# Zero products accumulated onto open PSUM groups at the end of the attention head, those groups spread further, and two reorderings

## The chip, the cores and the metric

The kernel runs as one program on one core of a Trainium2 chip. The metric is the device time of the execution in microseconds (us). The core has five engines with instruction streams of their own: TensorE (PE in the profile, with its weight loads as PEld), VectorE (DVE), ScalarE (ACT), GpSimd (POOL) and SyncE (SP), which here only issues transfers. Each engine takes its instructions in the order of its stream, and semaphores order the engines among each other.

## The reference

Three layers follow each other: causal attention with a decay bias over 2 batches of 8 heads (576 positions, head size 64), a leaky two-matrix MLP over the 1152 tokens (512 to 2048 to 512), and four small experts whose outputs are weighted and summed.

```python
scores = scale * np.matmul(q, k.transpose(0, 1, 3, 2))
cum = np.cumsum(np.maximum(s, 0.0), axis=-1)
bias = -(cum[:, :, :, None] - cum[:, :, None, :])
scores = np.where(causal, -1000000000.0, scores + np.minimum(bias, 0.0))
attn = softmax(scores)                      # written out in the original
x = np.matmul(attn, v)                      # to (1152, 512)
h = x @ w_in
x = np.maximum(0.01 * h, h) @ w_out         # to (1152, 512)
for e in range(4):
    out += p[:, e:e + 1] * (np.maximum(x @ w1[e], 0.0) @ w2[e])
```

The weights `w_in` and `w_out` come as 64-bit numbers and are converted to 32 bits on the chip.

## The kernel before

**Order of the work.** Every instruction goes through a small wrapper (`issue`, line 43, which is why nearly every row of the profile reads L43). While its flag `fixed` is true, the instructions stay in the order in which the Python code is run; after the line `fixed = False` a scheduler may reorder them.

**The head.** Attention is cut into 16 units, each two heads of one batch and either the first two tiles of 128 queries (units 0 to 7, "the head") or the last three (units 8 to 15). The generator `attention` counts items `i` (one tile of one head), and each item passes through five steps with lags: `scores` (products into `ps_sc`, then a DVE reduction into `z` and `mn`), `exps` (ACT, lag 1), `transposes` (PE into `ps_pt`, then an ACT copy to `pv`, lag 3), `values` (PE into `ps_o`, after the unit's last item the DVE's `st` and `xo`, lag 5) and `finish` (PE into `ps_x`, then ACT and DVE into `x0`, lag 7). `ps_o` has one buffer, so the next unit's first `values` waits for the `xo` of the unit before. Between the steps the loop weaves other work: while `i < 20` two products of a zero tile (`idling(2)`, into a bank `nothing` of their own); from `i = 22` one step of `opening` at a time, three products of 512 columns of the first MLP into one of three `ps_u` banks that stay open over four rounds; and `units_of_w`, the conversion of the weights on ACT and DVE (`raw`, `w`). The head's loop ends when unit 7 is finished, at `i = 38`. `split_keys` (`qs`, `ks`, `kd`) prepares the keys of units 8 to 15 on ACT and DVE.

**First loads.** `cumulative` issues the first transfers on SP: the row of `s`, keys and queries of units 0 and 1, their values `vs`, and the two rows of the cumulated sum (`decay`, `ke<-cum`), one for each of the two halves `l` of its split.

**The MLP in two sets of tokens.** The first MLP is done for the first 512 tokens (`phases[0]`, woven into the attention) and then for the other 640 (`phases[1]`, the second set), in four blocks each. A block has two up steps and one down step, in the order that `in_order` gives. In the second set an up step (`paired_up`) forms 4x4 blocks of a product from 7 products in place of 8: its weights are a "seven" (`w7`, made by POOL sums, an ACT copy as the high part and a POOL difference as the low part; two buffers), its results fill four PSUM banks, which ACT and DVE turn into the hidden tile `ht`. A down step (`down1`) has 8 groups of 12 products of 320 columns into `ps_d`, with two weight tiles `w` (three buffers). Two sevens are made ahead of the second set. The order of the steps there is up b0 first, up b0 second, up b1 first, down b0, up b1 second, up b2 first, down b1, and so on. This stretch is scheduled, not fixed.

Of the kernel before, what the change touches and what calls it, by code (L numbers as in the profile page):

```python
# [9 lines left out]
F32 = mybir.dt.float32  # L10
# [9 lines left out]
def attention_moe_moe2(ctx: ExitStack, tc: tile.TileContext, q, k, v, s, w_in, w_out, probs, w1, w2, out):  # L20
# [30 lines left out]
    B, H, D, S = q.shape  # L51
# [3 lines left out]
    P = 128  # L55
# [19 lines left out]
    def f32(ap):  # L75
        return ap.bitcast(F32)
# [161 lines left out]

    def in_order(blocks):


        for i in range(len(blocks) + 1):
            if i < len(blocks):
                yield "up", blocks[i], 0
            if i > 0:
                yield "down", blocks[i - 1], None
            if i < len(blocks):
                yield "up", blocks[i], 1

# [63 lines left out]
    def opening(h):  # L313

        w = next_w(2)
        ps = [ps_mm.tile([P, 512], F32, tag="mm", name="ps_u") for _ in range(3)]
        for kk in range(KD):
            for i in range(3):
                wi, sl = w[i // 2], slice(i % 2 * P, (i % 2 + 1) * P)
                for j, (l, m) in enumerate(((0, 0), (1, 0), (0, 1))):  # L320
                    nc.tensor.matmul(ps[i], wi[:, l, kk, sl], x_t[0][:, m, kk], start=(kk == j == 0), stop=(kk == KD - 1 and j == 2))
                if kk == KD - 1:
                    evict_up(ps[i], h)
                yield
        yield from up1(w[1], h, (1,))
# [162 lines left out]
    ps_mm = banks.enter_context(tc.tile_pool(name="ps_mm", bufs=3, space=PSUM))  # L488
# [9 lines left out]
    cum2 = nothing = None  # L498
    idle = ap.tile([P, P], F32, name="idle", bufs=1)
# [3 lines left out]
    def cumulative():  # L503

        nonlocal cum2
        pos, cum = (r64p.tile([P, 2048], F32, tag="r64", name=n)[:BH] for n in ("pos", "cum"))
        spos, zero, cum = pos[:, :S], pos[:, S : 2 * S], cum[:, :S]
        nc.sync.dma_start(spos, s)
        nc.vector.memset(idle, 0.0)
        nc.vector.memset(zero, 0.0)  # L510
        idling(22)
        load_keys(0)
        load_values(0)
        load_keys(1)
        cum2 = early.tile([BH, 2, S], F32R, name="cum2")
        for lo, hi in ((0, half[0]), (half[0], S)):
            part = slice(lo, hi)
            nc.vector.tensor_scalar(spos[:, part], spos[:, part], 0.0, D ** 0.5, ALU.max, ALU.mult)
            nc.vector.tensor_tensor_scan(cum[:, part], spos[:, part], zero[:, part], cum[:, lo - 1 : lo] if lo else 0.0, ALU.add, ALU.add)
            nc.scalar.copy(cum2[:, 0, part], cum[:, part])  # L520
            nc.vector.tensor_tensor(cum2[:, 1, part], cum[:, part], f32(cum2[:, 0, part]), ALU.subtract)
            if lo == 0:
                decay(0, k_e[0])
                load_values(1)
                decay(1, k_e[1])
        nc.sync.dma_start(cum_d.rearrange("l h k -> h l k"), f32(cum2))

    def idling(n):

        for _ in range(n):  # L530
            nc.tensor.matmul(nothing[:, :P], idle, idle, start=True, stop=True)


    v_s = [ap.tile([P, QT, 2 * D + 2], F32, tag=f"v{i}", name="vs", bufs=1) for i in range(4)]
# [53 lines left out]
    def load_values(n):  # L588
        b, hp, i0, i1 = of_unit(n)
        q1, rows, vs = tiles[i1 - 1][2], slice(hp * P, (hp + 1) * P), v_s[n % 4]  # L590
        full = min(q1 // P, QT - 1)
        nc.sync.dma_start(vs[:, :full, 1 : 2 * D + 1], v[b, : full * P, rows].rearrange("(t p) c -> p t c", p=P))
        if i1 == QT:
            nc.sync.dma_start(vs[P - S % P :, QT - 1, 1 : 2 * D + 1], v[b, full * P :, rows])
# [19 lines left out]
    def decay(n, kd):  # L614

        b, hp, i0, i1 = of_unit(n)
        q1, h = tiles[i1 - 1][2], b * H + 2 * hp
        if n < 2:
            for l in range(2):
                nc.sync.dma_start(kd[D + l : D + l + 1], f32(cum2[h : h + 2, l, :q1]))  # L620
        else:
            nc.sync.dma_start(f32(kd[D:DK, :, :q1]), cum_d[:, h : h + 2, :q1])

# [88 lines left out]
    def attention():  # L712

        nonlocal ending
        items, starts, n = [], {}, 0
        i, split = 0, iter(())
        while n < units or i < len(items) + 7:
            if n < units and i == len(items):
                u = Unit(n)
                starts[n] = i  # L720
                items += [(u, *of) for of in u.items]
                if n + 2 < units and n + 2 != 2 * NP:
                    load_keys(n + 2)
                    if n + 2 < 2 * NP:
                        decay(n + 2, k_e[(n + 2) % 3])
                if n + 3 == 2 * NP:
                    load_keys(n + 3)
                n += 1
            if n < units - 1 and i == starts[n - 1] + 2:
                load_values(n + 1)  # L730
            if i == starts[n - 1] + 2 and 2 * NP - 1 <= n < units and n != 2 * NP:
                split = split_keys(max(n, 2 * NP))
            for step, lag in STEPS:
                if 0 <= i - lag < len(items):
                    u, *of = items[i - lag]
                    ending = step == Unit.exps and 0 <= i - 5 < len(items) and items[i - 5][1:] == items[i - 5][0].items[-1]
                    step(u, *of)
                if lag == 1:
                    next(split, None)
                if lag in (1, 3, 7):  # L740
                    yield i
            i += 1
# [9 lines left out]
    with ExitStack() as phase:  # L752
        x_t[0] = phase.enter_context(tc.tile_pool(name="x0pool", bufs=1)).tile([P, 2, KD, sizes[0]], F32R, name="x0")
        wpool = phase.enter_context(tc.tile_pool(name="wpool", bufs=4))
        r64p = phase.enter_context(tc.tile_pool(name="r64p", bufs=2))
        side, units_of_w, late, opened = attention(), supply(), late_splits(), 0
        nothing = ps_mm.tile([P, 512], F32, tag="mm", name="nothing")
        with tc.tile_pool(name="early", bufs=1) as early:
            ones = pads(early)
            cumulative()  # L760
            main = mlps(phases[0])

            for at_ in range(3 * 64):
                i = next(side)
                if done == 2 * NP:
                    break
                if at_ % 3 == 0 and i in (6, 8):
                    nc.scalar.copy(q_s[i // 2 - 3][D:DK, 1], ones[D:DK])
                if at_ % 3 == 1:
                    if i < 20:  # L770
                        idling(2)
                    elif i >= 22 and opened < 3 * (done // 2) and (opened < 6 or i >= 30):
                        next(main)
                        opened += 1
                if at_ % 3 == 2:
                    if i in (1, 5):
                        fetch64(i // 4)
                    if i >= 8 and (i < 21 or i >= 29):
                        next(units_of_w)
        hidden_pool(phase, 6)  # L780

        owed = 0
        for at_, i in enumerate(side):
            if at_ % 3 < 2:
                owed += WOVEN * KD / (2.0 * (48 - 6))
                while owed >= 1.0:
                    next(main)
                    owed -= 1.0
            if at_ % 3 != 1:
                next(late, None)  # L790
            if at_ % 3 == 2 or at_ % 3 == 0 and not ending:
                next(units_of_w, None)
        attn.close()
        w7pool = ctx.enter_context(tc.tile_pool(name="w7pool", bufs=2, side="right"))
        scratch = ctx.enter_context(tc.tile_pool(name="scratch", bufs=2, side="right"))
        t7pool = ctx.enter_context(tc.tile_pool(name="t7pool", bufs=1, side="right"))
        tokens = paired_steps(1, x_t[1], t7pool)
        banks.close()
        ps_mm = ctx.enter_context(tc.tile_pool(name="ps_all", bufs=8, space=PSUM))

        sevens = first_sevens()
        for m, _ in enumerate(main):
            if m % 2 == 0:
                next(late, None)
            if m % 4 == 0:
                next(tokens, None)
            if m % 4 == 2:
                next(units_of_w, None)
            if m % 4 % 2 and m >= 4:
                next(sevens, None)  # L810
        for _ in sevens:
            pass
        for _ in tokens:
            pass
# [57 lines left out]
```

## Time and profile before

| What | Value |
|---|---|
| Time, median of 3 runs | 746.86 us (744.03 to 746.86) |
| The profiled execution: its own time, its span | 739.91 us, 738.1 us |
| Mean granted TensorE clock over the span | 0.992 of 2.4 GHz |
| PE busy | 715.0 us, 97% of the span |
| PEld, DVE, ACT, POOL busy | 88%, 58%, 45%, 39% |
| Chain that ended last | PE 87%, DVE 5%, ACT 3%, issue 2% |

The profiled execution is 1.8 us longer than its span, and 7 us shorter than the median of the unprofiled runs. PE is the engine that is busy nearly everywhere; its idle time sits in the first 250 us and at one place behind 257 us.

### The profile page before, as it was taken

Reading aid. Unit: us, or ns where it says so; the run is one execution under the profiler, and the core shown is the slowest. Engines: PE = TensorE matmul, PEld = TensorE weight load, DVE = VectorE, ACT = ScalarE, POOL = GpSimd, SP = SyncE. Lnnn points to the kernel's source line nnn. Section 1 sums busy time; section 2 is a strip of 40 time slices with the busy share of each in tenths; the row PEclk is TensorE's granted clock in tenths of the full one; section 3 lists DMA queues with packets and bytes.
Section 4 is the critical chain, followed back from the end, with each engine's and each line's share of the span. In section 5 each row is a group of like instructions: output and inputs, shape, how many; then the busy total and the mean of one; then the engine's idle time right before and its main releaser. Section 6 shows DMA issues by size and latency. Waiting matters only on the chain.

```text
span 738.1 us, 11412 instructions
## 1 busy us (share of the span) xinstructions
PE 715.0 (97%) x4388; PEld 650.6 (88%) x4388; DVE 428.2 (58%) x866; ACT 330.8 (45%) x643; POOL 286.7 (39%) x234
## 2 busy tenths in 40 slices
PE   9998899999999989999999999999999999999997
PEld 9886788888888889999988988989889898898986
DVE  4858797889737735853874544634436444454442
ACT  5767978786654556453531422413324133132210
POOL 4111121211228788885163372522714327053200
PEclk9999999999999999999999999999999999999999
DMA  6775567765432222131020110202103011020012
GB/s 167 216 217 152 158 195 239 247 212 184 169 114 87 87 86 86 58 115 58 1 87 30 57 59 18 69 29 58 57 1 86 29 58 58 0 58 1 1 38 90
DMA packets 40745, 68.85 MB, mean 93 GB/s; under 512 B 3988, under 2 KB 22964, under 8 KB 40692
## 3 DMA queue, kind: packets, MB, share of 16 engines
q1 hardware_dynamic: 31988, 42.97, 19.7%
q10 hardware_dynamic: 8704, 25.17, 9.9%
q8 instruction: 34, 0.56, 0.3%
q14 instruction: 19, 0.16, 0.1%
HBM read 57.30 MB, written 10.82 MB: 92 GB/s over the span
## 4 chain that ended last, share of the span: by engine, by line
PE 87%; DVE 5%; ACT 3%; issue 2%; DMA 1%; ACTq 0%; DVEq 0%; SPq 0%
PE ps_d L43 40%; PE ps_u L43 34%; PE ps_o L43 5%; PE ps_sc L43 3%; PE ps_pt L43 3%; DVE raw L43 2%; PE nothing L43 2%; DMA raw<-w_f 1%; DVE t L43 1%; ACT pv L43 1%; ACT ps_u L43 1%; PE ps_x L43 1%; DVE z L43 0%; ACTq L43 0%; ACT ht L43 0%
## 5 line engine op out<-in xcount | busy, mean ns | idle before, releaser
L43 POOL TENSOR_TENSOR w<-raw,w 128x1024 fp32r<-128x1024 f32 (+2 forms) x88 | 147.5, 1693 | 395.7 <-ACT w L43 395.7
L43 PE MATMUL ps_u<-t,w 128*128 128x320 f32 (+1 forms) x1680 | 237.5, 299 | 4.1 <-ACT w L43 3.0
L43 PEld LDWEIGHTS ps_u<-t,w 128*128 128x128 f32 x1680 | 233.5, 190 | 8.3 <-ACT w L43 3.5
L43 PE MATMUL ps_d<-w,ht 128*128 128x512 f32 x864 | 203.3, 391 | 0.0
L43 PEld LDWEIGHTS ps_d<-w,ht 128*128 128x128 f32 x864 | 160.2, 188 | 31.9
L43 ACT ACTIVATE ht<-ps_u 128x320 fp32r<-128x320 f32 (+2 forms) x176 | 74.1, 432 | 159.6 <-DVE ps_u L43 129.1
L43 PE MATMUL ps_d<-ht,w 128*128 128x320 f32 (+1 forms) x576 | 111.4, 343 | 0.9 <-DVE y L43 0.9
L43 DVE SCALAR_TENSOR_TENSOR oacc<-ps_d,pn,oacc 128x512 f32<-128x512 f32 x63 | 47.3, 751 | 104.3 <-PE ps_d L43 104.3
L43 ACT CAST w<-raw 128x1024 fp32r<-128x1024 f32 (+2 forms) x88 | 63.9, 756 | 87.1 <-PE ps_d L43 71.5
L43 PEld LDWEIGHTS ps_d<-ht,w 128*128 128x128 f32 x576 | 92.1, 191 | 6.7 <-ACT t L43 1.3
L43 PEld LDWEIGHTS ps_o<-vs,pv 128*128 128x128 f32 x480 | 64.2, 193 | 13.1 <-issue 6.4
L43 DVE TENSOR_TENSOR ps_u<-ps_u,tmp 128x320 f32<-128x320 f32 (+1 forms) x120 | 56.4, 471 | 26.7 <-PE ps_u L43 25.3
L43 DVE SCALAR_TENSOR_TENSOR ht<-ps_u,ht 128x320 fp32r<-128x320 f32 (+1 forms) x128 | 56.3, 452 | 23.3 <-ACT ht L43 22.0
L43 PE MATMUL ps_o<-vs,pv 128*128 128x65 f32 x480 | 63.7, 269 | 6.2 <-issue 3.9
L43 DVE TENSOR_TENSOR tmp<-ps_u,tmp 128x320 f32<-128x320 f32 (+1 forms) x80 | 36.9, 464 | 47.4 <-PE ps_u L43 40.5
L43 POOL TENSOR_TENSOR w<-sums,w 128x1024 fp32r<-128x1024 f32 x24 | 58.8, 2451 | 9.5 <-ACT w L43 9.5
L43 PE MATMUL ps_u<-x,w 128*128 128x512 f32 x192 | 57.4, 414 | 0.0
L43 ACT ACTIVATE z<-z,mn 128x256 f32<-128x256 f32 (+4 forms) x80 | 48.6, 608 | 16.6 <-DVE mn L43 15.0
L43 DVE CUSTOM_DVE_ANT_0 z<-ps_sc,mask 128x256 f32<-128x256 f32 (+4 forms) x80 | 40.8, 512 | 20.5 <-PE ps_sc L43 14.1
L43 ACT COPY pv<-ps_pt 128x512 f32<-128x512 f32 (+3 forms) x96 | 38.9, 423 | 19.8 <-PE ps_pt L43 19.4
L43 PE MATMUL ps_pt<-ident,z 128*128 128x128 f32 x240 | 41.6, 282 | 5.5 <-ACT pv L43 5.5
L43 DVE TENSOR_TENSOR ht<-ps_u,ht 128x320 fp32r<-128x320 f32 (+1 forms) x48 | 26.4, 555 | 31.0 <-ACT ps_u L43 30.9
(72 smaller groups left out, 624.9 us busy)
## 6 DMA issues: line engine op xcount, KB each, us to landing
raw<-in_moe_w_dram SPq DMA_DIRECT2D x32, 512.0 KB, 3.5
raw<-w_f SPq DMA_DIRECT2D x25, 512.0 KB, 4.2
r<-in_moe_w_in_dram ACTq DMA_DIRECT2D x8, 1024.0 KB, 8.8
w_f<-raw ACTq DMA_DIRECT2D x16, 512.0 KB, 3.0
r<-in_moe_w_out_dram ACTq DMA_DIRECT2D x8, 1024.0 KB
qr<-in_q_dram SPq DMA_DIRECT2D x16, 160.0 KB, 4.2
kr<-in_k_dram SPq DMA_DIRECT2D x8, 288.0 KB, 8.5
vs<-in_v_dram SPq DMA_DIRECT2D x8, 256.0 KB, 4.9
```

The lines of the kernel that those rows point to most:

```text
L43: ins = call(*args, **kw)
```

## The change

There are five edits. (1) From `i = 31` to the head's end, each item gets two products of the zero tile (`onto_held`), added with `start=False` to the open bank of `opening`'s third group, so that they add zero to what it holds. (2) The nine steps of `opening` that fall into the head's loop are issued at the items of a table `OPENED` in place of at 22 to 27 and 31 to 33. (3) In the second set, the down step of block 0 comes ahead of the first up step of block 1. (4) The values of units 0 and 1 are loaded behind the rows of the cumulated sum. (5) The second row of each of these goes out on ACT's queue.

```diff
     def in_order(blocks):
         for i in range(len(blocks) + 1):
+            down = [("down", blocks[i - 1], None)] if i > 0 else []
+
+            if i == 1 and blocks[0][2] == 1:
+                yield from down
+                down = []
             if i < len(blocks):
                 yield "up", blocks[i], 0
-            if i > 0:
-                yield "down", blocks[i - 1], None
+            yield from down
             if i < len(blocks):
                 yield "up", blocks[i], 1
...
-        ps = [ps_mm.tile([P, 512], F32, tag="mm", name="ps_u") for _ in range(3)]
+        ps = held[:] = [ps_mm.tile([P, 512], F32, tag="mm", name="ps_u") for _ in range(3)]
...
         load_keys(0)
-        load_values(0)
         load_keys(1)
...
             if lo == 0:
-                decay(0, k_e[0])
-                load_values(1)
-                decay(1, k_e[1])
+                for n in range(2):
+                    decay(n, k_e[n])
+                    load_values(n)
...
+    def onto_held():
+
+        nc.tensor.matmul(held[2][:, :P], idle, idle, start=False, stop=False, skip_group_check=True)
...
-            for l in range(2):
-                nc.sync.dma_start(kd[D + l : D + l + 1], f32(cum2[h : h + 2, l, :q1]))
+            for l, queue in enumerate((nc.sync, nc.scalar)):
+                queue.dma_start(kd[D + l : D + l + 1], f32(cum2[h : h + 2, l, :q1]))
...
+        OPENED = (22, 23, 25, 27, 28, 30, 32, 34, 36)
...
-                    elif i >= 22 and opened < 3 * (done // 2) and (opened < 6 or i >= 30):
+                    elif opened < len(OPENED) and i >= OPENED[opened] and opened < 3 * (done // 2):
                         next(main)
                         opened += 1
+                if at_ % 3 < 2 and i >= 31:
+                    onto_held()
```

**The second set, PE's stream.** Before, behind the last six products of block 0's second up step (`ps_u3_2791`, weights `w7_2613`), stand the first products with the third seven (`w7_2708`), and then those of the down step (`ps_d`, weights `w_2783`).

```order
L43 MATMUL ps_u3_2791<-t7_1_2488,w7_2613 128x320 x5
L43 MATMUL ps_u0_2859<-t7_1_2488,w7_2708 128x320 [waits DVE_49,Activation_49]
L43 MATMUL ps_u1_2860<-t7_1_2488,w7_2708 128x320 [waits DVE_49,Activation_49]
L43 MATMUL ps_u2_2861<-t7_1_2488,w7_2708 128x320 [waits DVE_49]
L43 MATMUL ps_u3_2862<-t7_1_2488,w7_2708 128x320 [waits DVE_49]
L43 MATMUL ps_d_2952<-ht_2715,w_2783 128x320 [waits DMAHW4_49,DMAHW0_49,DMAHW6_49,DVE_49,PE_49]
L43 MATMUL ps_d_2952<-ht_2715,w_2783 128x320 [waits Pool_49]
```

With the change the same place (now `ps_u3_2798`) is followed by the down step alone, on the hidden tiles `ht_2722` and `ht_2793` of block 0; its 96 products stand there without a product of an up step among them.

```order
L43 MATMUL ps_u3_2798<-t7_1_2504,w7_2629 128x320 x5
L43 MATMUL ps_d_2888<-ht_2722,w_2719 128x320 [waits DMAHW4_49,DMAHW6_49,DMAHW0_49,DVE_49]
L43 MATMUL ps_d_2888<-ht_2722,w_2719 128x320 [waits Pool_49]
L43 MATMUL ps_d_2888<-ht_2722,w_2719 128x320 [waits DVE_49]
L43 MATMUL ps_d_2902<-ht_2722,w_2719 128x320 [waits Activation_49]
L43 MATMUL ps_d_2902<-ht_2722,w_2719 128x320
L43 MATMUL ps_d_2916<-ht_2722,w_2719 128x320 [waits DVE_49]
L43 MATMUL ps_d_2916<-ht_2722,w_2719 128x320 x2
```

Four product rows with the third seven have gone from there. Three up steps in a row now stand behind the down step: with the seven `w7_2868`, with `w7_2880`, and with the third, `w7_3017`, which takes the buffer of the first. The last products with `w7_2868` are those of `ps_u3_3029`; PE's stream of the change goes on behind them:

```order
L43 MATMUL ps_u2_3099<-t7_1_2504,w7_2880 128x320 x6
L43 MATMUL ps_u3_3100<-t7_1_2504,w7_2880 128x320 x6
L43 MATMUL ps_u0_3097<-t7_1_2504,w7_2880 128x320 [waits Activation_49]
L43 MATMUL ps_u0_3097<-t7_1_2504,w7_2880 128x320 x5
L43 MATMUL ps_u0_3168<-t7_1_2504,w7_3017 128x320 [waits DVE_49,Activation_49]
L43 MATMUL ps_u2_3099<-t7_1_2504,w7_2880 128x320 [waits DVE_49]
L43 MATMUL ps_u2_3099<-t7_1_2504,w7_2880 128x320 x5
L43 MATMUL ps_u3_3100<-t7_1_2504,w7_2880 128x320 [waits DVE_49]
L43 MATMUL ps_u3_3100<-t7_1_2504,w7_2880 128x320 x5
L43 MATMUL ps_u1_3169<-t7_1_2504,w7_3017 128x320 [waits Activation_49]
L43 MATMUL ps_u2_3170<-t7_1_2504,w7_3017 128x320
L43 MATMUL ps_u3_3171<-t7_1_2504,w7_3017 128x320 [waits DVE_49]
```

18 products of the second seven stand between the last product with the first and the first with the third, and 12 more ahead of the next; the row behind these is the first that waits for POOL's low part of the third seven. From the down step of block 1 on, the streams of all engines are those of before but for names.

**The head, PE's stream, items 30 to 32.** Before, from the last `values` of item 30 on (`ps_x` is the `finish` of unit 5):

```order
L43 MATMUL ps_o<-vs,pv 128x65 x2
L43 MATMUL ps_x<-ident,xo 128x128 x2
L43 MATMUL ps_sc<-ke_116,qe_115 128x128
L43 MATMUL ps_pt<-ident,z 128x128 x2
L43 MATMUL ps_u<-x_102,w 128x512 x3
L43 MATMUL ps_o<-vs,pv 128x65
L43 MATMUL ps_sc<-ks,qs 128x448
```

With the change, the same stretch:

```order
L43 MATMUL ps_u<-x_102,w 128x512 x3
L43 MATMUL ps_o<-vs,pv 128x65 x2
L43 MATMUL ps_x<-ident,xo 128x128 x2
L43 MATMUL ps_sc<-ke_116,qe_115 128x128
L43 MATMUL ps_u<-idle 128x128
L43 MATMUL ps_pt<-ident,z 128x128 x2
L43 MATMUL ps_u<-idle 128x128
L43 MATMUL ps_o<-vs,pv 128x65
L43 MATMUL ps_sc<-ks,qs 128x448
```

The step of `opening` that stood behind `ps_pt` of item 31 has moved ahead of the `values` of item 30, and the zero products (`ps_u<-idle`) stand around `ps_pt`. There are 16 of them in all, two in each of the items 31 to 38. Steps now stand at items 34 and 36 as well.

## Rows read from the trace of the kernel before

In the rows of windows the columns are the stretch and its length, the busy time of PE, PEld, DVE, ACT and POOL (with instructions), the granted clock as a share of 2.4 GHz, the DMA share and GB/s. In the rows of the timeline they are start, duration, engine, operation, tiles, shapes and count, with the idle time before and what ended it in brackets. A float32 product of the zero tile, a transpose or a product of `ps_o` shows as two records.

**Rows 1.** Windows of 10 us.
```profile
60.00:70.00 10.00, 7.16 (x38) 5.29 (x37) 9.04 (x17) 8.21 (x16) 2.98 (x1) 0.83 0.83 242
250.00:260.00 10.00, 7.85 (x53) 7.43 (x51) 7.09 (x16) 6.09 (x16) 5.28 (x3) 1.00 0.34 105
260.00:270.00 10.00, 9.16 (x52) 9.09 (x52) 0.99 (x3) 5.10 (x12) 9.18 (x10) 0.83 0.35 107
```

**Rows 2.** Waits of PE over the span: us in total, times, longest.
```profile
PE ps_pt L43 <- ACT pv L43: 5.5, 7, 1.7
```

**Rows 3.** Timeline of PE at the beginning of the second set.
```profile
245.03 12.48 PE L43 MATMUL ps_u<-t,w 128*128 128x320 f32 x84
259.66 0.41 PE L43 MATMUL ps_u<-t,w 128*128 128x320 f32 x1 [2.15 <-ACT w L43]
260.91 0.71 PE L43 MATMUL ps_u<-t,w 128*128 128x320 f32 x3 [0.84 <-ACT w L43]
261.45 4.02 PE L43 MATMUL ps_d<-ht,w 128*128 128x320 f32 x17
```

**Rows 4.** Windows of 1 us with a lower granted clock.
```profile
51.00:52.00 1.00, 1.00 (x6) 1.00 (x6) 0.07 (x2) 0.16 (x1) 0.00 (x0) 0.50 0.91 234
...
263.00:264.00 1.00, 1.00 (x6) 1.00 (x5) 0.49 (x1) 0.02 (x1) 1.00 (x1) 0.50 0.58 123
```

**Rows 5.** Timeline of ACT at the same place.
```profile
257.64 0.43 ACT L43 ACTIVATE ht<-ps_u 128x320 fp32r<-128x320 f32 x1
...
259.00 0.92 ACT L43 CAST w<-raw 128x512 fp32r<-128x512 f32 x2
259.81 1.05 ACT L43 CAST w<-sums 128x1024 fp32r<-128x1024 f32 x1
```

**Rows 6.** Timeline of POOL around the second set's beginning.
```profile
234.57 1.87 POOL L43 TENSOR_TENSOR sums<-sums,raw 128x256 f32<-128x256 f32 x1
...
262.03 2.38 POOL L43 TENSOR_TENSOR w<-sums,w 128x1024 fp32r<-128x1024 f32 x1
264.37 1.98 POOL L43 TENSOR_TENSOR w<-raw,w 128x512 fp32r<-128x512 f32 x2
266.29 1.45 POOL L43 TENSOR_TENSOR sums<-raw 128x256 f32<-128x256 f32 x2
```

**Rows 7.** Timeline of DVE, the sums of tokens for later sevens.
```profile
278.30 0.94 DVE L43 TENSOR_TENSOR sums<-y 128x256 f32<-128x256 f32 x1
...
280.71 1.02 DVE L43 TENSOR_TENSOR t<-y,t 128x512 fp32r<-128x512 f32 x2
```

**Rows 8.** Timeline of PE in the head, where it waited.
```profile
49.82 0.63 PE L43 MATMUL ps_o<-vs,pv 128*128 128x65 f32 x4 [1.84 <-issue]
...
58.71 0.49 PE L43 MATMUL ps_sc<-ks,qs 128*128 128x512 f32 x1 [0.75 <-DVE mn L43]
...
64.22 1.26 PE L43 MATMUL ps_pt<-ident,z 128*128 128x128 f32 x5 [1.72 <-ACT pv L43]
...
68.46 1.30 PE L43 MATMUL ps_o<-vs,pv 128*128 128x65 f32 x10 [0.82 <-PE ps_pt L43]
```

**Rows 9.** The chain in order of time: start, us, what.
```profile
27.92 0.45 PE nothing L43 x4
...
55.25 0.69 PE ps_u L43 x3
```

**Rows 10.** Timeline of DVE in the head.
```profile
49.30 0.42 DVE L43 TENSOR_TENSOR xo<-ps_o,st 128x256 f32<-128x256 f32 x1
...
61.11 0.42 DVE L43 TENSOR_TENSOR x<-ps_x,x 128x256 fp32r<-128x256 f32 x1 [0.83 <-ACT x L43]
```

**Rows 11.** Timeline of PE at the start.
```profile
1.06 7.66 PE L43 MATMUL nothing<-idle 128*128 128x128 f32 x44 [1.06 <-DVE idle L43]
8.56 0.60 PE L43 MATMUL ps_sc<-ke,qe 128*128 128x256 f32 x2
```

**Rows 12.** Timeline of SP's queue at the start.
```profile
5.78 1.41 SPq L43 DMA_DIRECT2D ke<-cum  x2
```

More of the change, by code (lines that the diff above doesn't have):

```diff
@@ L531, in idling @@
             nc.tensor.matmul(nothing[:, :P], idle, idle, start=True, stop=True)
+    held = []
+    def onto_held():
+        nc.tensor.matmul(held[2][:, :P], idle, idle, start=False, stop=False, skip_group_check=True)
     v_s = [ap.tile([P, QT, 2 * D + 2], F32, tag=f"v{i}", name="vs", bufs=1) for i in range(4)]
```

## Prediction, made before the changed kernel ran

> **What bounds the kernel now.** I read the page first: PE is busy for 97% of the span, so only idle time of PE, a clock below full, or added or removed products can move the end. The slices then show where PE idles: in the first 250 us and once behind 257 us. From 270 us on its slices are full; time saved at 257 us reaches the end one for one, since nothing behind it offers slack.
>
> The windows of 10 us show that place with its price: PE busy for 7.85 of 250 to 260, then 9.16 of 260 to 270 at a granted clock of 0.83 [rows 1]. The timeline of PE says what happens. 84 products of block 0 take 12.48 us, 0.149 us each, and end at about 257.5. The next product needs the high part of the third seven and waits 2.15 us for ACT; the one behind it waits 0.84 us for the copy of its sums; the down step begins only at 261.45 [rows 3]. ACT's timeline says why it is late: the hidden tiles of block 0 and other copies stand ahead of those two copies, which start at 259.00 and 259.81 [rows 5]. So the stretch from 257.53 to 261.45 holds 3.92 us and four products (0.59 us): 3.33 us lost. After it the granted clock falls: 0.83 over 260 to 270 is 1.7 us lost [rows 1], with 0.50, which is 1.2 GHz, in the window at 263 [rows 4]. In all the place costs **5.0 us**.
>
> The other place is the head. From item 31 on (about 58 us) PE waits for DVE and ACT in turn, 0.75, 1.72 and 0.82 us in the rows shown [rows 8]; over the span its waits for `pv` come to 5.5 us in 7 places [rows 2]. The clock falls twice: at about 50.9 for some 3.1 us (three windows, of which one is shown, near 0.50 [rows 4]: 1.6 us of work), behind the wait of 1.84 us at 49.8 [rows 8], and at 64.3 for 3.3 us, behind the wait of 1.72 us (0.83 over 60 to 70 is 1.7 us [rows 1]). But in the head DVE is the engine that is busy for 9.04 of 10 us, against 7.16 of PE [rows 1], so neither fall costs its whole 1.6 or 1.7 us.
>
> **The second set's order (edit 3).** It adds and removes no work. Behind the 84 products there are now 96 products of the down step in a row, 14.3 us. Their weights were cast before; of the hidden tiles only the last parts are open. The stream's first such wait is for the ACT tile that starts at 257.64 and takes 0.43 us [rows 5], reached after three products at 257.98: a wait of some 0.1 us, and I allow 0.2. The later tiles have 6 products or more between them, and ACT and DVE have at this place the work that they had. So the 3.33 us go but for 0.2, and with the idle time, which went ahead of the fall of the clock, I take the fall as gone: 3.33 + 1.70 - 0.2 = **4.8 us gained**. The lower bound is 3.1 us (the clock falls later all the same).
>
> What is late next? Three up steps now follow each other. The third takes the buffer of the first seven, so ACT can copy its high part only after the last product with that one. By the stream this is product 150 from the start of the down step, at 257.7 + 150 x 0.149 = 280.0; the new high part is wanted 18 products, 2.7 us, later, the copy of the sums 12 products behind that (1.9 us with the step's own), and the low part of POOL at product 184, at 285.1. ACT needs 0.92 and 1.05 us for its two copies [rows 5], which fits. POOL is closer. It comes free at 264.41 [rows 6] and has in its stream, ahead of that last low part, two halves' low parts (1.98 each time), two sets of sums (four of 0.73, 2.9 each) and three full low parts (2.4 each) [rows 6], in all 17.0 us: 281.4, with an estimated 1.8 us of waiting for ACT's copies 283.2. The slack is 1 to 2 us. I cost this at nothing in the likeliest case; without the cover it is the first rival.
>
> **The head (edits 1 and 2).** The zero product is priced by its kin: the chain shows 0.45 us for four records, two products, so **0.22 us each** at full clock [rows 9]; 16 of them are 3.6 us, and 7.1 us at half clock. An opening step is three products, 0.69 us [rows 9]; there are nine before and after, so moving them adds nothing by itself. Most of the zero products lie in idle time of PE: the three waits shown behind item 31 are 3.3 us [rows 8]. Those that don't are the ones ahead of a `finish`. DVE's `x` at 61.11 waits 0.83 us for ACT's copy of `ps_x` [rows 10], so whatever stands ahead of `ps_x` there is on the path: two zero products, 0.45 us, and the same once more at unit 7's `finish`, another 0.45 us. On the gaining side, two steps fewer stand ahead of the wait at 49.8, but that wait is for DVE's `xo`, which starts at 49.30 whatever PE does [rows 8, 10]; it stays. If the first fall of the clock disappears I count 0.3 us of its 1.6, the part for which DVE had no work of its own; the second is free, since PE waits for DVE again at 68.46 [rows 8]. Sum: 0.45 + 0.45 - 0.3 = **0.6 us lost**. Bounds: both falls disappear and all of it comes back, 0.9 - 3.3 = 2.4 us gained; or the first fall stays and the step that now stands ahead of `ps_x` of item 30 runs at half clock, 2 x 0.69 = 1.4 us more on the path: 2.0 us lost.
>
> **First loads (edits 4 and 5).** PE's idle products run to 8.72 and the first scores start at 8.56 without a wait [rows 11]. What the change shortens is SP's queue, where the two rows `ke<-cum` take 1.41 us [rows 12]: nothing waits for their issue as long as PE has its idle products. I take 0; without that cover it is at most half the row, 0.7 us. The Trainium skill ("DMA: Bandwidth & Descriptors", Issuing engines are not separate DMA queues) says that transfers issued from several engines share the same 16 DMA engines, so that only the issuer's time is saved; by that the edit brings those 0.7 us and no bandwidth, and no run here shows more yet.
>
> **Sum.** -4.8 + 0.6 + 0 = -4.2 us. The profiled execution took 739.91 us itself, so 735.7; it stands 6.95 us under the median of the runs shown, a difference that I can't explain from the trace and carry along. Against the median: 746.86 - 4.2 = **742.7 us**, 0.56% less.
>
> **The rivals.**
>
> *A, as above:* 742.7 us. Chance 0.45.
>
> *B, the third seven is late.* DVE's sums of tokens, from 278.30 to 281.73 before [rows 7], follow the down step, and so run earlier in the change, beside POOL's sums. Where both worked before, one of POOL's sums took 1.87 us in place of 0.73 [rows 6]. With two to three such stretchings POOL is 2.3 to 3.6 us later and eats the 1 to 2 us of slack. PE then waits some 2.4 us at product 184: 742.7 + 2.4 = 745.1, and 746.8 if the clock falls there as it did at 262. Against it: only a few operations of DVE meet POOL's. Chance 0.18. The Trainium skill ("SBUF — State Buffer", Who interferes with whom) speaks for this rival: a VectorE operation with two SBUF inputs shuts out a GpSimd one that reads SBUF for its whole length; the sum of 1.87 us agrees.
>
> *C, the other side: the zero products stand on the head's path.* They wait in PE's order for nothing, but what is behind them (transposes and values for ACT and DVE) waits for them. The point of decision is 4.8 / 16 = 0.30 us a product: at full clock (0.22 us, 3.6 us) the change still gains 1.2 us, at half clock all 7.1 us on the path make 746.86 - 4.8 + 7.1 = 749.2, slower. For it: the clock has been at half at this very place [rows 1, 8]. Against it: PE idles there for 3.3 us. Chance 0.12.
>
> *D, the head gains too.* The zero products fill the idle time that goes ahead of both falls, the clock stays up, and the transposes and values come sooner to DVE and ACT: -4.8 - 2.4 = -7.2, 739.7 us. For it: both falls come behind a wait of over 1.7 us [rows 8]; against it: DVE's 9.04 of 10 us [rows 1], and that the wait at 49.8 lies ahead of the first zero product. Chance 0.25.
>
> **How the numbers follow.** The likeliest is A, 742.7, by itself 741.5 (half of what D would bring the head) to 744.4 (the place at 257 by its lower bound). The range 738.0 to 747.5 holds A, B and nearly all of D; it leaves out C and some of D and B, about 2 in 10. A difference of 0.5% (3.7 us, 743.1) is about what a measurement of this kernel tells from no change, its runs spread over 2.8 us. Faster by more than that: D almost whole, 0.24, and six in ten of A, which straddles the bound, 0.27, with 0.02 of B: 0.53. Slower by more than 0.5%: most of C, 0.09. The rest, 0.38, lies within.
>
> **What would show it right or wrong.** In the changed trace PE should go from `ps_u` to `ps_d` at about 257 us with no wait over 0.3 us, and the windows behind it should read 1.00 in the clock; if a fall stands there or later, 1.7 us of the gain are gone. At the first product with the third seven's low part, some 27 us behind, a wait for POOL's or ACT's `w` shows B. In the head, the start of PE's last `ps_x` and the first opening steps behind the loop, compared with before, give edits 1 and 2 directly: 0.6 us later is A, 2 us earlier is D, 3 us later is C. `ps_sc` at 8.56 should not move. The prediction fails most easily if the head's timing follows PE more than DVE's busy share lets me think, or if some wait far behind the second set takes back what the place at 257 gives.

## The result, and the profile after

The change is faster: 738.27 us median of 10 executions (736.34 to 740.89) against 745.63 of 10 before (739.5 to 747.28), ratio 0.9908 with a 95% interval of 0.9882 to 0.9933, that is 6.9 us or 0.92%. The forecast was 742.7, in a range of 738.0 to 747.5: the result lies 0.3 us inside the range's lower end, and nearer to rival D (739.7) than to the forecast.

The profiled execution of the change took 740.89 us, the longest of the ten, and that of before 739.91, nearly the shortest. Their spans (739.1 and 738.1 us) can't be compared as wholes; their stretches can.

**The second set.** The timeline of PE after the change (start, duration, tiles, shapes, count, and idle time in brackets, of which there is none here) answers to [rows 3]:

```profile
250.71 12.49 PE L43 MATMUL ps_u<-t,w 128*128 128x320 f32 x84
263.04 14.45 PE L43 MATMUL ps_d<-ht,w 128*128 128x320 f32 x96
277.32 13.92 PE L43 MATMUL ps_u<-t,w 128*128 128x320 f32 x93
291.08 4.42 PE L43 MATMUL ps_d<-ht,w 128*128 128x320 f32 x29
```

The 84 products run into the 96 of the down step, and these into the three up steps, with no row of waiting. In the windows (columns as in [rows 1]; the first two are the head's) PE is busy throughout from 260 on, and the clock is at 1.00, which is 2.4 GHz:

```profile
60.00:70.00 10.00, 7.64 (x54) 6.95 (x54) 7.93 (x15) 8.66 (x15) 2.86 (x1) 1.00 0.62 206
70.00:80.00 10.00, 9.08 (x68) 8.37 (x66) 7.95 (x21) 6.27 (x12) 0.00 (x0) 1.00 0.27 65
...
260.00:270.00 10.00, 10.00 (x69) 9.80 (x68) 6.30 (x13) 8.49 (x21) 6.74 (x5) 1.00 0.41 139
270.00:280.00 10.00, 10.00 (x71) 10.00 (x70) 5.94 (x7) 5.33 (x10) 8.76 (x8) 1.00 0.18 65
```

From the first of the 84 products to the end are 738.1 - 245.03 = 493.1 us before [rows 3] and 739.1 - 250.71 = 488.4 after: **4.7 us** gained here. The profiled executions of the experiments agree: this stretch takes 488.4 to 489.3 us in all eleven that have edit 3 and 492.9 to 493.1 in the three that don't, 4.3 us apart in the mean.

**The head.** The same 84 products begin 5.7 us later in the profiled change, and the last `ps_x` of the head, the prediction's own sign, starts at 75.15 against 71.76 before: 3.4 us later, where 0.6 was to be A and 3 was to be C. So these two executions say that everything ahead got slower. The waits of PE, for [rows 2]:

```profile
PE ps_pt L43 <- ACT pv L43: 9.9, 7, 2.9
```

2.7 us of that is one wait that before doesn't have at this place. The timeline of ACT shows its cause, a load of queries that came late:

```profile
45.65 0.72 ACT L43 CAST qs<-qr 128x640 fp32r<-128x640 f32 x1 [2.88 <-DMA qr<-in_q_dram]
```

PE's wait in the profiled change, and in another profiled execution of it (e11, below), whose 84 products begin at 248.93:

```profile
46.59 0.44 PE L43 MATMUL ps_pt<-ident,z 128*128 128x128 f32 x2 [2.72 <-ACT pv L43]
...
46.08 0.44 PE L43 MATMUL ps_pt<-ident,z 128*128 128x128 f32 x2 [0.91 <-ACT pv L43]
```

Its length is that execution's own, its place is not: of the profiled executions with the first six steps of `opening` moved, eight of nine wait here, 0.35 to 2.72 us, and of the five with them at the old items none does. There one more step stood ahead of these transposes, which suggests that edit 2 lets PE arrive before ACT, held up by the queries, has copied `pv`. The start of PE is as it was, the first scores 0.12 us earlier than in [rows 11]:

```profile
1.06 7.54 PE L43 MATMUL nothing<-idle 128*128 128x128 f32 x44 [1.06 <-DVE idle L43]
8.44 0.60 PE L43 MATMUL ps_sc<-ke,qe 128*128 128x256 f32 x2
```

One execution of each kernel doesn't decide what the head gained: the stretch from the last `ps_x` to the 84 products, the work of which no edit changes, takes from 173 to 180 us in the profiled executions. But every timed execution comes with its span and its mean granted clock, and (1 - clock) x span is the work, in time at full clock, that PE could not do. Where PE would have waited anyway, none of it reaches the end. In the profiled execution of before (0.992) that is 5.9 us; over 84 timed ones of before that ran beside the experiments it is 9.9 us on average, from 3.7 to 14.2. The experiments are read by this.

### The profile page after: what moved, and what is told of

Same layout as the page of the kernel before. It is cut to its first block, busy times and chain, and to the rows that moved or that the text cites. A ratio compares the mean times of both kernels' runs of the same rounds, so it can differ in the third digit from the quotient of the medians.

```text
span 739.1 us, 11479 instructions
## 1 busy us (share of the span) xinstructions
PE 715.3 (97%) x4420; PEld 651.7 (88%) x4420; DVE 434.1 (59%) x866; ACT 330.9 (45%) x643; POOL 288.4 (39%) x234
## 4 chain that ended last, share of the span: by engine, by line
PE 88%; DVE 5%; ACT 3%; issue 2%; DMA 1%; SPq 0%; ACTq 0%; DVEq 0%
PE ps_d L43 40%; PE ps_u L43 34%; PE ps_o L43 5%; PE ps_sc L43 3%; PE ps_pt L43 3%; PE nothing L43 2%; DVE raw L43 2%; DMA qr<-in_q_dram 1%; DVE z L43 1%; DVE t L43 1%; PE ps_x L43 1%; ACT pv L43 1%; ACT ps_u L43 1%; ACT ks L43 0%; ACT ht L43 0%
## 5 line engine op out<-in xcount | busy, mean ns | idle before, releaser
L43 PE MATMUL ps_d<-ht,w 128*128 128x320 f32 (+1 forms) x576 | 109.9, 340 | 0.9 <-DVE y L43 0.9
L43 PEld LDWEIGHTS ps_pt<-ident,z 128*128 128x128 f32 x240 | 29.8, 141 | 18.3 <-ACT pv L43 12.0
```

What stands on the lines that cost most here:

```text
L43: ins = call(*args, **kw)
```

## The experiments

All times are in us. "Lost" is (1 - clock) x span, "rest" the time less that; both are means over the n executions of the kernel. The times scatter by 1.3 to 3.4 us (standard deviation), the rest by 0.5 to 1.5, so the differences of times below come with 95% intervals. The column "ratio" is the measurement's own estimate against the executions of before beside the run; it differs from the quotient of the means by up to 0.2%. The runs fall into three groups on three chips, on which before took 745.1, 744.9 and 745.1 in the mean, so runs of different groups are compared.

```
run                    edits            n  median  ratio (95%)              mean   lost  rest
before                 none            84  745.64                          745.0    9.9  735.1
change                 all             10  738.27  0.9908 (0.9882-0.9933)  738.2    1.3  736.9
e11_change_again       all             12  739.22  0.9924 (0.9904-0.9945)  739.5    2.2  737.2
e1_order_only          3               12  741.29  0.9956 (0.9929-0.9983)  740.9    8.3  732.6
e2_all_but_order       1,2,4,5         12  742.90  0.9988 (0.9956-1.0020)  743.9    4.5  739.4
e3_loads_only          4,5             12  745.73  0.9999 (0.9968-1.0029)  744.4    9.2  735.3
e4_no_zero             2,3,4,5          6  737.55  0.9915 (0.9884-0.9947)  737.6    4.2  733.4
e12_no_zero_again      2,3,4,5          8  738.49  0.9918 (0.9888-0.9948)  738.7    4.8  733.9
e5_old_steps           1,3,4,5         12  740.27  0.9941 (0.9914-0.9969)  740.3    3.9  736.4
e6_zero_half           all, 8 of 16    12  739.22  0.9932 (0.9903-0.9961)  739.3    2.8  736.5
e9_zero_x2             all, 32 of 16    7  740.27  0.9935 (0.9908-0.9962)  740.0    1.3  738.7
e7_first_six_spread    3,4,5, part 2   12  742.55  0.9956 (0.9921-0.9991)  741.2    7.8  733.5
e8_last_three_spread   3,4,5, part 2   12  739.30  0.9920 (0.9892-0.9949)  738.7    6.3  732.4
e10_even_steps         3,4,5, other 2   6  737.84  0.9908 (0.9879-0.9938)  737.9    4.2  733.8
```

**Edit 3 alone, and all but edit 3.** The first is the kernel before with the new `in_order`, the second the change with the old one:

```diff
+            if i == 1 and blocks[0][2] == 1:
+                yield from down
+                down = []
```

> Only edit 3, the down step of block 0 ahead of the first up step of block 1; the rest is the kernel before. Theory: the two traces show 493.1 us from the first product of the second set to the end before and 488.4 after, so edit 3 alone is worth 4.7 us, ratio 0.9937, and its trace shows the clock at 1.00 behind the place. Rival: part of the gain there comes with the head's edits (other phase of POOL and DVE), then under 3 us, ratio above 0.996.

> The change without edit 3. Theory: the head's and the loads' edits bring what is left of the measured 6.9 us, some 2.2 us, ratio 0.997; the 3.4 us that the profiled execution of the change lost up to item 38 are that execution's own (late keys and queries), and this run's trace loses less. Rival: they cost, as the profiled execution says, 3 us or more, ratio 1.004 or above; then edit 3 must have brought more than its own place shows.

Edit 3 alone gains 4.1 us of mean time (interval 2.8 to 5.5; 3.3 by the ratio), of which 1.6 in lost clock and 2.5 in the rest; its trace has 735.8 - 247.11 = 488.7 us from the first of the 84 products on, as the change has. Without edit 3 the stretch is 740.7 - 247.79 = 492.9 us again and both waits are back. First e1, then e2 with its window from 260 on:

```profile
247.11 12.49 PE L43 MATMUL ps_u<-t,w 128*128 128x320 f32 x84
```

```profile
247.79 12.48 PE L43 MATMUL ps_u<-t,w 128*128 128x320 f32 x84
...
262.33 0.42 PE L43 MATMUL ps_u<-t,w 128*128 128x320 f32 x1 [2.06 <-ACT w L43]
263.58 1.17 PE L43 MATMUL ps_u<-t,w 128*128 128x320 f32 x3 [0.83 <-ACT w L43]
```

```profile
260.00:270.00 10.00, 7.11 (x37) 6.61 (x37) 2.47 (x5) 6.55 (x16) 9.51 (x8) 0.83 0.35 107
```

The theory holds for edit 3. What e2 gains, 0.9 us by the ratio with an interval from -1.5 to +3.3, rules out that the other edits cost 3 us, but leaves their share open by itself: its lost clock is halved (9.9 to 4.5), its rest 4.3 us longer. On top of edit 3 they gain 2.0 us (0.5 to 3.5): 740.9 in e1, 738.9 over both runs of the change.

**The loads.** Edits 4 and 5 on the kernel before:

```diff
         load_keys(0)
-        load_values(0)
...
-                decay(0, k_e[0])
-                load_values(1)
-                decay(1, k_e[1])
+                for n in range(2):
+                    decay(n, k_e[n])
+                    load_values(n)
...
-            for l in range(2):
-                nc.sync.dma_start(kd[D + l : D + l + 1], f32(cum2[h : h + 2, l, :q1]))
+            for l, queue in enumerate((nc.sync, nc.scalar)):
+                queue.dma_start(kd[D + l : D + l + 1], f32(cum2[h : h + 2, l, :q1]))
```

> Only edits 4 and 5, the first loads. Theory: nothing waits for them, 0 within 1 us, ratio 0.999 to 1.001, the first scores at 8.5 us. Rival: the earlier end of SP's queue carries the later loads of keys and queries, so that ACT's copy of the queries comes sooner: 1.5 us or more, ratio 0.998 or below.

Nothing that can be seen, 0.9999 (0.9968 to 1.0029, some 2.3 us to either side). The rival's gain of 1.5 us lies inside that interval. The worth of this run is its profiled execution, which is one of the common long ones of the old head (span 744.5, clock 0.985; the mean over the 84 of before is 0.987). Its windows and its PE timeline at the head's end:

```profile
60.00:70.00 10.00, 6.16 (x37) 4.49 (x35) 8.87 (x17) 8.32 (x15) 2.98 (x1) 0.86 0.81 228
70.00:80.00 10.00, 10.00 (x44) 9.54 (x44) 4.62 (x13) 3.78 (x8) 0.00 (x0) 0.50 0.07 25
```

```profile
64.80 0.76 PE L43 MATMUL ps_pt<-ident,z 128*128 128x128 f32 x5 [1.72 <-ACT pv L43]
...
67.11 1.09 PE L43 MATMUL ps_pt<-ident,z 128*128 128x128 f32 x4 [0.98 <-ACT pv L43]
69.04 2.37 PE L43 MATMUL ps_o<-vs,pv 128*128 128x65 f32 x10 [0.84 <-PE ps_pt L43]
...
73.25 2.23 PE L43 MATMUL ps_o<-vs,pv 128*128 128x65 f32 x10
```

Here the clock fell behind the waits of 1.72 and 0.98 us and stood at 0.50, 1.2 GHz, through the whole window from 70 to 80, with PE busy for all of it and DVE for 4.62 of 10. The ten `ps_o` records (five products) took 2.37 us at half clock; in e1 they take 1.30. This is the second fall of the prediction, but it begins at 67.2 in place of 64.3 and costs 6.8 us of PE's work (from windows of 5 us) in place of 1.7, and now ACT and DVE wait for PE:

```profile
73.54 0.59 ACT L43 COPY pv<-ps_pt 128x512 f32<-128x512 f32 x1 [2.82 <-PE ps_pt L43]
75.94 0.37 ACT L43 CAST x<-ps_x 128x256 fp32r<-128x256 f32 x1 [1.81 <-PE ps_x L43]
```

In the trace of e1, whose head differs from this one by the loads alone, the clock is back before:

```profile
60.00:70.00 10.00, 7.17 (x41) 5.31 (x39) 8.84 (x17) 8.36 (x15) 2.99 (x1) 0.83 0.71 223
70.00:80.00 10.00, 9.98 (x70) 8.88 (x69) 6.45 (x17) 8.25 (x14) 0.13 (x1) 1.00 0.35 106
```

**The zero products.** None, half of them, twice as many (none also a second time, beside the change on one chip):

```diff
-                if at_ % 3 < 2 and i >= 31:
-                    onto_held()
...
-                if at_ % 3 < 2 and i >= 31:
+                if at_ % 3 == 0 and i >= 31:
...
                     onto_held()
+                    onto_held()
```

> The change without edit 1, no zero products. Theory (the head gains by the clock, rival D of the prediction): without them the clock falls again behind the head's waits, for some 3 us, and 1.7 to 2.2 us of the gain are gone: ratio 0.993 to 0.994. Rival (their 0.9 us on the path outweighs it, case A): it is 0.5 to 1 us faster than the change, ratio 0.990. If the steps' new places alone carry the head's gain, the same as the change, 0.991.

> The change with 8 zero products in place of 16, one ahead of each item's transposes from item 31 on. Theory: each zero product is on the head's path with its whole 0.22 us (the time without the lost clock went up by 3.5 us for 16), so that time falls by 1.75 us against the change; if half of them still hold the clock (lost clock up to 2 us) the kernel is 1 us faster than the change, 737.2. Rival: half of them don't hold it, lost clock 4.2 us as with none, 739.3. Second rival: they lie in waits and their cost is not their own; then the time without the lost clock stays at 736.9.

> The change with 32 zero products in place of 16, two where it has one. So far (means): the change loses 1.3 us to the clock and takes 736.9 without that; 16 products fewer: 4.2 and 733.4; 8 fewer: 2.8 and 736.5. Theory (each product is on the path with its own 0.22 us): the time without the lost clock goes up by another 3.5 us, the lost clock can't fall by more than 1.3, so 740.5 to 741.7 us. Rival (what the zero products add is not their own time but waits that stand where the slow clock stood, since DVE and ACT set the pace there): the time without the lost clock stays within 1 us of 736.9, and the kernel within 1 us of the change, 737.3 to 739.3.

> The change itself, beside the next run on the same chip: 738.2 us, lost clock 1.3.

> The change without its zero products once more, with more executions. Theory: the zero products give back in waits what they save in clock, so this is within 0.3% of the change beside it, 737.5 us, lost clock 4.2. Rival: they are worth 1 us or more, then this is at 739.5 or above.

They do hold the clock: in all six profiled executions with zero products it reads 1.00 from 60 to 80 us, in all eight without it falls there. The first fall they don't reach: e6 has the clock at 0.66 from 50 to 60, the profiled change 0.85 from 40 to 50. Without them, as in e4:

```profile
60.00:70.00 10.00, 6.73 (x44) 5.23 (x44) 8.71 (x15) 8.50 (x15) 2.86 (x1) 1.00 0.64 196
70.00:80.00 10.00, 10.00 (x52) 9.32 (x52) 6.09 (x16) 5.48 (x10) 0.00 (x0) 0.66 0.25 57
```

And they bring nothing that can be seen by it. The change's second run came out 1.3 us above its first (739.5 after 738.1). Over both runs of each, the change takes 738.9 and the change without them 738.2, a difference of 0.6 with an interval from -0.7 to +2.0: the third of e4's outcomes and the theory of e12. Lost clock falls by 2.8 (4.5 to 1.8), the rest grows by 3.4 (733.7 to 737.1). Neither theory on that growth is right as it stood: if each product cost its own 0.22 us, 0, 8, 16 and 32 of them would add 0, 1.8, 3.6 and 7.1 to the rest; measured are 0, 2.8, 3.4 and 5.0. The first eight cost more than themselves, the last sixteen 1.6 of their own 3.5 (0.4 to 2.8). One place where two stand wholly on the path can be read, from the last scores ahead of unit 7's `ps_x` to it: 72.38 - 70.19 = 2.19 us in e1, 75.15 - 72.48 = 2.67 in the change, 0.48 us more, their 0.44. First e1, then the change:

```profile
70.19 0.45 PE L43 MATMUL ps_sc<-ks,qs 128*128 128x448 f32 x1
...
72.38 0.39 PE L43 MATMUL ps_x<-ident,xo 128*128 128x128 f32 x2
```

```profile
72.48 0.45 PE L43 MATMUL ps_sc<-ks,qs 128*128 128x448 f32 x1
...
75.15 0.39 PE L43 MATMUL ps_x<-ident,xo 128*128 128x128 f32 x2
```

What the zero products are worth depends on the fall that they meet. From unit 5's `ps_x`, just ahead of the first of them, to unit 7's, the head takes 20.35 us before and 20.37 in e1, without them and with a second fall that is short; 20.53 in e5, with them, the old steps and no fall; 20.88 in e11, with them, the new steps and no fall; 22.95 in e3, without them and with the long fall. In this order:

```profile
51.41 0.63 PE L43 MATMUL ps_x<-ident,xo 128*128 128x128 f32 x2
71.76 0.39 PE L43 MATMUL ps_x<-ident,xo 128*128 128x128 f32 x2
...
52.01 0.63 PE L43 MATMUL ps_x<-ident,xo 128*128 128x128 f32 x2
72.38 0.39 PE L43 MATMUL ps_x<-ident,xo 128*128 128x128 f32 x2
...
50.06 0.39 PE L43 MATMUL ps_x<-ident,xo 128*128 128x128 f32 x2
70.59 0.39 PE L43 MATMUL ps_x<-ident,xo 128*128 128x128 f32 x2
...
52.62 0.39 PE L43 MATMUL ps_x<-ident,xo 128*128 128x128 f32 x2
73.50 0.39 PE L43 MATMUL ps_x<-ident,xo 128*128 128x128 f32 x2
...
52.33 0.63 PE L43 MATMUL ps_x<-ident,xo 128*128 128x128 f32 x2
75.28 0.63 PE L43 MATMUL ps_x<-ident,xo 128*128 128x128 f32 x2
```

So in these executions keeping the clock up pays against the long fall, by some 2.4 us, and brings nothing against the short one (e5 to e1: 0.16 us longer). Each is one execution. How the 3.4 us divide between the products' own time and lost clock that never reached the end was not settled.

**The opening steps.** Old places with the zero products; then, without zero products, only the first six moved, only the last three, and nine at nearly even distances:

```diff
-                    elif opened < len(OPENED) and i >= OPENED[opened] and opened < 3 * (done // 2):
+                    elif i >= 22 and opened < 3 * (done // 2) and (opened < 6 or i >= 30):
...
-        OPENED = (22, 23, 25, 27, 28, 30, 32, 34, 36)
+        OPENED = (22, 23, 25, 27, 28, 30, 31, 32, 33)
...
+        OPENED = (22, 23, 24, 25, 26, 27, 32, 34, 36)
...
+        OPENED = (22, 24, 26, 28, 30, 32, 34, 36, 37)
```

> The change without edit 2: the opening steps at their old items (22 to 27, 31 to 33), zero products kept. So far the lost clock (one less the granted clock, times the span, mean over the timed executions) is 9.8 us before, 8.3 with edit 3 alone, 4.2 with the change but its zero products, 1.3 with the change. Theory: steps and zero products act on the same falls of the clock, behind item 31, and either is enough for most of them; then the lost clock is 1.3 to 3 us here and the time 738.5 to 740.5, ratio 0.991 to 0.993. Rival: the steps act on other falls than the zero products, and the parts add up: lost clock 5.4 us, time 742 to 743, ratio 0.995 to 0.997.

> The change without its zero products (737.55 us, lost clock 4.2), and of the nine steps only the first six at their new items (22 to 30), the last three at 31 to 33 as before. Theory: the steps at 34 and 36 stand where PE waits for ACT and hold the clock; without them the lost clock goes back to 8.3 us, the time to 741.3. Rival: the first six, which no longer make PE run ahead into the wait at 49.8, carry it: lost clock 4.2, time 737.6.

> The same with the first six steps at their old items (22 to 27) and the last three at 32, 34 and 36. Theory: as the change without zero products, lost clock 4.2 us, 737.6. Rival: as before's steps, lost clock 8.3 us, 741.3.

> The change without its zero products, with the nine steps at 22, 24, 26, 28, 30, 32, 34, 36 and 37: one more late in the head. Theory: the later the last steps, the less clock is lost, as moving the last three alone took 2.0 us of it and all nine 4.2; lost clock 2 to 4 us, the time 736 to 737.5, at least as fast as the change. Rival: the steps of the change hit the falls by their places and not by being late; lost clock 6 us or more, 739 to 741.

Between edit 3 alone (740.9, lost 8.3) and the change without zero products (738.2, lost 4.5) lies edit 2, if the loads bring nothing: 2.7 us (interval 1.0 to 4.3), more than all of it in lost clock. With the zero products in place it is worth less, 1.4 us (-0.1 to 2.9, e5 against the change). Moving the last three steps to 32, 34 and 36 brings 2.2 of it (0.5 to 3.9), lost 6.3; moving the first six alone nothing that can be seen (0.3 us slower, between 2.6 slower and 2.0 faster). The traces point the same way: among the executions without zero products the long fall of some 13 us stands in e3 and again in e7 (clock 0.65 and 0.67 from 60 to 70 and 70 to 80), both with the last three steps at their old items, and in none of e4, e8, e10 and e12, which have them later; before and e1 have the old places and a short fall, so the places don't settle it in every execution. The even spacing is level with the change (0.9908), so it isn't these very items that count. e5 came out between its two expectations in lost clock: with the old steps the zero products save 4.4 us of clock and cost 3.8 of rest, a gain of 0.6 that its interval (-1.1 to 2.3) doesn't tell from none. Not all lost clock is the head's: the traces of e2, e5 and e7 also have a fall between 143 and 166 us. No version beat the change beyond the intervals; the one without zero products can't be told from it and has less code.

## Why the prediction came out so

**The second set: right, in mechanism and size.** -4.8 was forecast, -4.7 shows in the two traces, and edit 3 alone took 4.1 off the mean time; over all traces it is 4.3. The forecast wait of 0.2 us for the hidden tiles didn't appear; the clock's fall went with the idle time, as assumed.

**Rival B: fell, but narrowly.** A slack of 1 to 2 us had been forecast. PE's first product with POOL's low part of the third seven is the 89th of the three up steps, at about 277.32 + 88 x 0.148 = 290.3 ((291.08 - 277.32) / 93 each). POOL had the first half of that low part done at 288.85 + 1.31 = 290.16, and the second at 290.86, when PE had gone on. So the slack was 0.2 us or less; no wait shows. It went in two ways: POOL's waits for ACT's copies came to 1.16 + 1.55 us, where 1.8 had been estimated, and three of its sums took 1.80 + 1.19 us beside DVE's sums, as this rival says, where their kin took 1.44 + 0.74 later on, with no sums on DVE. The timeline of POOL in the change, the last row from a narrower window:

```profile
272.25 1.80 POOL L43 TENSOR_TENSOR sums<-raw 128x256 f32<-128x256 f32 x2
274.01 1.19 POOL L43 TENSOR_TENSOR sums<-sums,raw 128x256 f32<-128x256 f32 x1
...
277.24 2.42 POOL L43 TENSOR_TENSOR w<-sums,w 128x1024 fp32r<-128x1024 f32 x1 [1.16 <-ACT w L43]
...
281.99 1.44 POOL L43 TENSOR_TENSOR sums<-raw 128x256 f32<-128x256 f32 x2
283.38 0.74 POOL L43 TENSOR_TENSOR sums<-sums,raw 128x256 f32<-128x256 f32 x1
...
286.49 4.37 POOL L43 TENSOR_TENSOR w<-raw,w 128x1024 fp32r<-128x1024 f32 x3 [1.55 <-ACT w L43]
...
288.85 1.31 POOL L43 TENSOR_TENSOR w<-raw,w 128x512 fp32r<-128x512 f32 x1
```

**The loads: not contradicted.** 0 was forecast, 0.9999 measured, with 2.3 us of uncertainty.

**The zero products: near in the sum, in part by luck.** The two terms of 0.45 us gave 0.9; with and without them differ by 0.6 (-0.7 to 2.0), and the one place that could be read has 0.48. But the 0.6 is what is left of 3.4 us more rest and 2.8 less lost clock, and the sum had neither. Rival C's slow case needed them at half clock; from 60 to 80 us the clock doesn't fall while they are there. The prediction also has item 31 at about 58 us, but in before it begins behind unit 5's `ps_x` at 51.41, inside the first fall.

**The opening steps: the step that failed.** It is the sentence "If the first fall of the clock disappears I count 0.3 us of its 1.6, the part for which DVE had no work of its own; the second is free, since PE waits for DVE again at 68.46". The term was -0.3, and edit 2 is worth -2.7 without the zero products (1.0 to 4.3), -1.4 with them. It was sized on one execution with short falls, and on DVE's busy share in a window of 10 us. For such an execution nothing here contradicts it: before and e1 pass the head's end no later with a short fall (20.35 and 20.37 us from unit 5's `ps_x` to unit 7's) than e5 and e11 with none (20.53 and 20.88). In e3's execution of the same head the second fall stays for some 13 us, into a stretch in which DVE is busy for less than half and PE for all of the time, and nothing hides it. So 0.6 us lost in the head became some 2 us gained (0.5 to 3.5): the head gained nearly what rival D said, but the part of it that is clear of the noise is the steps', not the zero products'. The sign set for it, the last `ps_x` against before, misled for the same reason: e11 has it 1.7 us later than before, whose fall was short, and 1.8 us earlier than e3. Why the fall lasts in some executions and not in others stays open.

**The baseline.** 1.2 us of the 4.4 between forecast and result is the starting point: the forecast stood on a median of 746.86 over 3 runs, and 10 runs gave 745.63. The range held the result by 0.3 us; with the head mis-sized by 2.6 us, that is in part luck.

**The unexplained 6.95 us were a hint.** The prediction carried along, unread, that the profiled execution lay 6.95 us under the median. Its lost clock was 5.9 us, where the mean is 9.9: up to 4 us of that difference. A fall of varying length in a place that the change touches is a term of the sum.

## What to carry to other kernels

When a profiled execution is far from the median, ask for the clock and the span of the timed ones before a clock fall is priced by it: here the time lost to the clock ranged from 3.7 to 14.2 us in one program. The length of a fall decides what it costs: with the long one the head took 2.6 us more up to unit 7's `ps_x` than with the short one, and without the short one no less. Work that has to be done anyway, moved later in the head, brought 2.7 us; products of zeros kept the clock up as well and brought nothing that could be seen. A down step ahead of an up step whose weights are late cost no work and brought 4.1 us, because the weights' making was the last wait there.

## What the runs showed of the hardware

Between 70 and 80 us in e3's trace the granted clock stayed at 0.50 with PE's busy time at 10.00 of 10: there a busy row of PE didn't mean that the clock was back.

In the change's trace two of DVE's operations on `raw`, which take 1.22 us each where POOL rests, took 4.55 together while POOL's `w` ran beside them, which itself took 3.35 in place of 2.37. These timelines of DVE and POOL belong to the second half of the attention:

```profile
130.55 2.48 DVE L43 SCALAR_TENSOR_TENSOR raw<-r,raw 128x1024 uint32<-128x1024 uint32 x2
...
139.39 4.55 DVE L43 SCALAR_TENSOR_TENSOR raw<-r,raw 128x1024 uint32<-128x1024 uint32 x2
...
139.50 3.35 POOL L43 TENSOR_TENSOR w<-raw,w 128x1024 fp32r<-128x1024 f32 x1 [21.04 <-ACT w L43]
...
146.25 2.37 POOL L43 TENSOR_TENSOR w<-raw,w 128x1024 fp32r<-128x1024 f32 x1 [3.40 <-ACT w L43]
```

The Trainium skill ("SBUF — State Buffer", Who interferes with whom) says that a VectorE operation with two SBUF inputs and a GpSimd one that reads SBUF shut each other out for a whole instruction; these rows agree, and so does the sum of 1.87 us in [rows 6]. The change didn't bring this: before's trace has such a pair too, 4.05 at 135.97. How much of the scatter such meetings make was not measured.
